# Three edits to the attention half of a fused GateLoop and SwiGLU kernel: another queue for the first rotated q rows, later gate loads, and a scan per chunk and tile

## The chip, the cores and the metric

The kernel runs on one core of one Trainium2 chip. That core has TensorE (matrix products into PSUM), VectorE, ScalarE (activation functions, with tables that must be loaded), GpSimd, SyncE (which here only issues DMAs) and 16 DMA engines. The engines run at once, each through its own list of instructions in order, and wait for one another by semaphores. The metric is the device time of one execution in microseconds (us); lower is better.

## The reference, cut to what matters

A gated linear recurrence with complex gates, for 4 sequences of 768 steps with 8 heads of 48 features, and then a feed-forward network on its 3072 rows of 384. All inputs are float32 or, for the weights, wider numbers that the kernel narrows itself.

```python
mag = np.sqrt(a_re * a_re + a_im * a_im)
scale = np.minimum(mag, 0.999) / (mag + 1e-06)
a_re_n, a_im_n = (a_re * scale, a_im * scale)
for t in range(S):                                   # S = 768
    ar, ai = (a_re_n[:, :, t, :, None], a_im_n[:, :, t, :, None])
    new_re = ar * S_re - ai * S_im
    new_im = ar * S_im + ai * S_re
    kv = np.einsum('bhd,bhe->bhde', k[:, :, t], v[:, :, t])
    S_re, S_im = (new_re + kv, new_im)
    y[:, :, t] = np.einsum('bhd,bhde->bhe', q[:, :, t], S_re)
# ... y becomes x, 3072 x 384
xn = x / np.sqrt(np.mean(x * x, axis=-1, keepdims=True) + 1e-06) * rms_g
g = xn @ w_gate                                      # 384 x 1536
(g * (1 / (1 + np.exp(-g))) * (xn @ w_val)) @ w_out  # 1536 x 384
```

## The kernel before

The time axis is cut into 24 chunks of 128 steps. In a chunk, the running product of the gates is a magnitude and a phase: q is multiplied by the magnitude and turned by the phase, k is divided and turned, and then the chunk is ordinary attention, scores of 96 x 128 blocks masked with a triangle, plus a state that carries from chunk to chunk. Gates are prepared in *units*: units 0 and 1 have one chunk each, the other eleven have two. Rotated rows of q and k come out of VectorE with features of all heads mixed over 128 partitions, and are moved by DMAs (tile `ks`, `qs`, `k`, `q` to `kr`, `qr`) to a layout with one head's features on 96 partitions.

The program is emitted by a small list scheduler: each *lane* is a generator of steps with an engine, an estimated duration and the things it needs; at every turn the step that could begin first is emitted, with the lane's `late` added as a handicap and a table switch on ScalarE counted as extra. So a constant can reorder all engines. What is emitted is a fixed order for each engine.

```python
def begin(self, step, late):
    ...
    at = max(ready + self.HOP, self.clock.get(engine, 0.0))
    return at + (more["late"]() if "late" in more else late), at
# ... in run():
    switch = self.TABLE if table and self.table not in table else 0.0
    if best is None or found[0] + switch < best[0]:
        best = found[0] + switch, found[1], switch, lane
```

The loads of a unit's gates and rows, all on SyncE's queue but for the first two `im`:

```python
def load_gates():
    for u, (first_, m) in enumerate(units):
        for name, ap in (("re", a_re), ("im", a_im)):
            aside = u < 2 and name == "im"
            ...
            yield step("ACT" if aside else "SP", 0.0 if aside else 3 * order.ISSUE,
                       earlier(u, "moved3", 2) + ([("q", 1)] if u == 2 else []),
                       ..., mb=0.2 * m, ends=[(name, u)])
```

The gates of a unit: ScalarE and VectorE in turn; `w` holds the squared magnitudes, `p` their running products in each chunk:

```python
def products():
    wc = w.rearrange("p j (c t) -> p (j c) t", t=C)
    some = starts[:, 0:ND * m]                       # zeros, but for the first of each chunk
    nc.vector.tensor_copy(out=some[:, :, 0:1], in_=wc[:, :, 0:1])
    nc.vector.memset(wc[:, :, 0:1], 0.0)
    nc.vector.tensor_tensor_scan(out=flat(p), data0=flat(w), data1=flat(some),
                                 initial=0.0, op0=ALU.mult, op1=ALU.add)
# ... then roots, q * p, k * r, phase sums by scans, sine and cosine, and the rotation:
for i, (o, x, f) in enumerate((("ks", "k", s), ("qs", "q", s), ("k", "k", y), ("q", "q", y))):
    ... tt(t[o], t[x], f)                            # ends ("rot%d" % i, u)
```

The moves; ScalarE issues those of q for units 0 and 1:

```python
def move(i, ...):
    name, rows = ("kr", "qr")[i % 2], (1 - i // 2) * D
    queue = nc.scalar if u < ASIDE and i % 2 else nc.sync
    for j in range(ND):                              # ND = 3
        queue.dma_start(out=two[name][rows + j * L:rows + (j + 1) * L],
                        in_=t[("ks", "qs", "k", "q")[i]][:, j])
```

Weights come in 18 pieces of 768 KB on GpSimd's queue (`fetch`). A buffer is free again when VectorE has converted the piece before; GpSimd also waits for the piece two before to land (a copy into `behind`), and for the moved rows of units 0 and 1 ahead of pieces 3 and 4. Three operations of VectorE and one of ScalarE convert a piece (`narrow`). GpSimd also computes the power -0.5 of the row means (`rs`). TensorE fills gaps that the scheduler expects early on with matmuls on constants (`busy`), which keep its clock up and count for nothing.

The last part is `feed_forward`: for each of 12 groups of two chunks 12 tile pairs (`gv_ps`, 3 + 3 products) and then the output products (`out_ps`).

Of the kernel before, what the change touches and what calls it, by code (L numbers as in the profile page):

```python
# [24 lines left out]
ALU = mybir.AluOpType  # L25
# [3 lines left out]
P = 128  # L29
C = 128  # L30
# [15 lines left out]
class Order:  # L46
# [40 lines left out]
    def run(self):  # L87
        while self.lanes:
            best = None
            for lane in list(self.lanes):  # L90
                if lane[2] is None:
                    lane[2] = next(lane[0], None)
                    if lane[2] is None:
                        self.lanes.remove(lane)
                        continue
                found = self.begin(lane[2], lane[1])
                if found is None:
                    continue
                table = lane[2][4].get("table")
                switch = self.TABLE if table and self.table not in table else 0.0  # L100
                if best is None or found[0] + switch < best[0]:
                    best = found[0] + switch, found[1], switch, lane
            if best is None:
                assert not self.lanes, [x[2][:3] for x in self.lanes]
                return
            _, at, switch, lane = best
            engine, us, _, emit, more = lane[2]
            lane[2] = None
            self.gap = 0.0
            if engine == "PE" and (self.fill is None or self.fill not in self.ends):  # L110
                self.gap = min(at - self.clock.get("PE", 0.0), self.MOST)
                if more.get("fills") and self.gap > 1.5:
                    self.dense = self.WARM
            emit()
            pool, n = more.get("takes", (None, 0))
            if n:
                self.free[pool] = sorted(self.free[pool])[n:]
            if switch:
                self.table = more["table"][-1 if self.table == "silu" and "sigmoid" in more["table"] else 0]
            if engine == "PE":  # L120
                if at - self.clock.get("PE", 0.0) > self.GAP and not (more.get("fills") and self.gap):
                    self.dense = 0.0
                slow = self.dense < self.WARM
                self.dense += us if more.get("dense") else 0.0
                us = us * (1.9 if slow else 1.0)
            self.clock[engine] = end = at + us + switch
            if "mb" in more:
                queue = "POOL" if engine == "POOL" else "SP"
                self.moved[queue] = max(self.moved.get(queue, 0.0), at + 0.4) + more["mb"] / self.RATES[queue]
                end = self.moved[queue] + self.LAND  # L130
            end += more.get("then", 0.0)
            for k in more.get("ends", ()):
                self.ends[k] = end
            if "gives" in more:
                self.free[more["gives"]].append(end)


def step(engine, us, needs, emit, **more):
    return engine, us, needs, emit, more
# [429 lines left out]
def fast(tc, ctx, qT, kT, v, a_re, a_im, w_gate, w_val, w_out, rms_g, out, H, bad):  # L569

    nc = tc.nc
# [6 lines left out]
    ND = DM // P  # L578
    NF = DF // P
    UC = 2  # L580
    T = UC * C

    units = [(0, 1), (1, 1)] + [(n, UC) for n in range(2, N, UC)]
    NU = len(units)
    slots = [(0, 1)] + [(u,) for u in range(2, NU)]
# [17 lines left out]
    order = Order()  # L603
# [11 lines left out]
    def flat(x):  # L615
        return x.rearrange("p j t -> p (j t)")
# [15 lines left out]
    def earlier(u, what, by=1):  # L632

        k = max(u - 1, 0) - by
        return [(what, w) for w in slots[k]] if k >= 0 else []
# [23 lines left out]
    def filled(name, shape, value):  # L659
        t = consts.tile(shape, FP32, name=name)  # L660
        nc.gpsimd.memset(t, value)
        return t
# [21 lines left out]
    zero = filled("zero", [P, 1], 0.0)  # L684
    halfpi = filled("halfpi", [P, 1], PI / 2)
    round_ = filled("round_", [P, 1], ROUND)
    starts = filled("starts", [P, ND * UC, C], 0.0)
    causal = filled("causal", [C, C], 1.0)
    nc.gpsimd.affine_select(out=causal, in_=causal, pattern=[[1, C]], compare_op=ALU.is_ge,
                            fill=0.0, base=0, channel_multiplier=-1)  # L690
# [27 lines left out]
# [4 lines that stand above are left out]
                if (u, name) == (0, "im"):  # L722
                    order.ends[name, u] = 8.0
                    continue
                yield step("ACT" if aside else "SP", 0.0 if aside else 3 * order.ISSUE,
                           earlier(u, "moved3", 2) + ([("q", 1)] if u == 2 else []),
                           lambda name=name, ap=ap, u=u, q=nc.scalar if aside else nc.sync: gate(name, ap, q, u),
                           mb=0.2 * m, ends=[(name, u)])

# [23 lines left out]

    BEHIND = {3: ("piece", 7)}
    CHECK = 6
    LATE = 0.9
    WO = 1

    def gates(some):
        def E(engine, us, needs, emit, *names, **more):
            if u > 1:
                more["late"] = lambda: 0.1 if ("piece", 11) in order.ends else 0.2
            return step(engine, us, needs, emit, ends=names, **more)

        act_ = nc.scalar.activation
        for u in some:
            first_, m = units[u]
            t = UN[u]  # L770
            n1 = ND * m * C
            K = lambda x, u=u: (x, u)
# [5 lines left out]

            yield E("ACT", ac_us(n1), [K("re"), BEHIND.get(u)] + earlier(u, "rot"), begin, K("s0"))
            re, im, s, w, y, r, p, ks, qs = (t[x] for x in ("re", "im", "s", "w", "y", "r", "p", "ks", "qs"))  # L780
# [18 lines left out]

            def products():  # L800
                wc = w.rearrange("p j (c t) -> p (j c) t", t=C)
                some = starts[:, 0:ND * m]
                nc.vector.tensor_copy(out=some[:, :, 0:1], in_=wc[:, :, 0:1])
                nc.vector.memset(wc[:, :, 0:1], 0.0)
                nc.vector.tensor_tensor_scan(out=flat(p), data0=flat(w), data1=flat(some),
                                             initial=0.0, op0=ALU.mult, op1=ALU.add)

            yield E("DVE", 0.25 + n1 / 480, [], products, K("p2"))

            yield E("DVE", tt_us(n1), [K("abs")], lambda: tt(re, re, y))  # L810
            yield E("DVE", tt_us(n1), [], lambda: stt(im, re, 2.0, im, ALU.subtract, reverse0=True), K("tan"))
# [45 lines left out]
            for i, (o, x, f) in enumerate((("ks", "k", s), ("qs", "q", s), ("k", "k", y), ("q", "q", y))):  # L857
                more = [K("sin"), K("cos"), K("checked")]
# [3 lines left out]
    ASIDE = 2  # L862

    def move_rows():
        for u, (first_, m) in enumerate(units):
            t, two = UN[u], {}

            def move(i, t=t, u=u, two=two, first_=first_, m=m):
                name, rows = ("kr", "qr")[i % 2], (1 - i // 2) * D
                queue = nc.scalar if u < ASIDE and i % 2 else nc.sync  # L870
                if i < 2:
                    two[name] = sized(unit, name, H, m, p=D2)
                for j in range(ND):
                    queue.dma_start(out=two[name][rows + j * L:rows + (j + 1) * L],
                                      in_=t[("ks", "qs", "k", "q")[i]][:, j])
                for n in range(m) if i == 3 else ():
                    w = slice(n * C, (n + 1) * C)
                    U[first_ + n].update(k=two["kr"][:, :, w], q=two["qr"][:, :, w])

            for i in range(4):  # L880
                aside = u < ASIDE and i % 2
                yield step("ACT" if aside else "SP", 0.3 if aside else 3 * order.ISSUE,
                           [("rot%d" % i, u), ("y", units[u - 1][0] - 1) if u > 1 else None],
                           lambda i=i, move=move: move(i), mb=0.2 * m, then=order.MOVE,
                           ends=[("moved%d" % i, u)] + [("moved", u)] * (i == 3))
# [23 lines left out]
    parts = []  # L909
# [64 lines left out]
    def narrow(some):  # L974
# [3 lines left out]
        for i in some:  # L978
# [21 lines left out]
            def total(to=to.bitcast(I32), part=part):  # L1000
                tt(to, part["t"], to, ALU.add)

            more = dict(late=lambda i=i: (0.2 if i < 2 * NW else 0.3 if ("xT", 3) in order.ends else WO)
                        if ("rot", 1) in order.ends else LATE)
            yield step("ACT", 0.05 + ac_us(n), [("raw", i)], share, ends=[("share", i)], **more)
# [239 lines left out]
    order.lane(finish())  # L1245
    order.lane(scores(), 0.01)
    order.lane(load_gates(), 0.02)
    order.lane(load_rows(), 0.03)
    order.lane(move_rows(), 0.02)
# [1 line left out]
    order.lane(feed_forward(range(0, NG, 2)), 0.02)  # L1251
    order.lane(feed_forward(range(1, NG, 2)), 0.03)
    order.lane(gates([0]), 0.05)
    order.lane(gates(range(1, NU)), 0.2)
    order.lane(gains(), 0.1)
    order.lane(fetch(), 0.2)
    order.lane(narrow(range(0, len(parts), 2)), 0.3)
    order.lane(narrow(range(1, len(parts), 2)), 0.3)
    order.lane(small(), 0.5)
    order.fill = ("up", 1)  # L1260
# [7 lines left out]
    for to, in_, limit, op in ((ok[:, 0:ne], ends.rearrange("p u j c -> p (u j c)"), P_MIN, ALU.is_ge),  # L1268
# [9 lines left out]
                            op0=ALU.mult, op1=ALU.add)  # L1278
# [49 lines left out]
```

## Time and profile before

| | |
|---|---|
| time, median of 3 (lowest to highest) | 802.27 us (801.06 to 804.44) |
| span of the profiled execution | 798.4 us |
| busy: TensorE / VectorE / ScalarE / GpSimd | 735.0 / 424.3 / 341.7 / 43.5 us |
| first matmul | 26.84 us |
| first feed-forward tile; third | 71.35; 85.88 us |
| scores of chunk 2; of chunk 4 | 102.66; 171.43 us |
| last output product ends | 791.5 us |
| granted TensorE clock, mean | 0.977 |

The page sums busy time by engine and by slices of the span; the trace answers questions by time, and gives for each instruction how long its engine was idle before it and what ended that. TensorE does most of the work, so what is to be read is where it is not working on something useful, and what released it there. In names such as `s_ps<-qr,kr` the output stands left and the inputs right; s_ps are scores, kt_ps the transposed keys, state_ps the carried state, y_ps the attention's output.

### The profile page before, as it was taken

How to read it: one execution, taken by the hardware profiler on the slowest of the kernel's cores; microseconds unless marked ns; L12 is line 12 of the kernel's file. 1: busy time of each engine (PE TensorE's matmuls, PEld its weight loads, DVE VectorE, ACT ScalarE, POOL GpSimd, SP SyncE). 2: the span in 40 equal slices, each digit the busy share in tenths (PEclk: the TensorE clock that was granted, in tenths of full speed). 3: DMA queues.
4: the chain of work that ended last, by engine and by line, in shares of the span. 5: the costliest groups of instructions: out<-in, count | busy, mean ns of one | idle time of the engine just before them, and what ended most of it. 6: DMA issues, size and time to landing. Idle time of an engine off the chain costs nothing.

```text
span 798.4 us, 11801 instructions
## 1 busy us (share of the span) xinstructions
PE 735.0 (92%) x4728; PEld 589.0 (74%) x4728; DVE 424.3 (53%) x762; ACT 341.7 (43%) x548; POOL 43.5 (5%) x83
## 2 busy tenths in 40 slices
PE   0558989969999999999999999999999999999996
PEld 0345776857688977878878987779887778876783
DVE  4759678848395776657484756758212303320130
ACT  6455276645566647365537557454111101110110
POOL 3010122101000000000000000000000000000000
PEclk9968999989999999999999999999999999999999
DMA  8692992690847438290927556094700114301510
GB/s 225 85 220 65 156 260 80 104 193 12 117 93 84 95 44 156 38 141 12 163 37 94 96 66 112 27 175 119 99 1 1 60 50 128 119 10 51 177 40 24
DMA packets 99775, 76.46 MB, mean 96 GB/s; under 512 B 39041, under 2 KB 90497, under 8 KB 99713
## 3 DMA queue, kind: packets, MB, share of 16 engines
q1 hardware_dynamic: 93760, 60.30, 41.4%
q0 software_dynamic: 3360, 14.16, 6.3%
q10 hardware_dynamic: 2592, 1.18, 1.0%
q8 instruction: 39, 0.64, 0.4%
q14 instruction: 24, 0.19, 0.1%
HBM read 51.98 MB, written 4.76 MB: 71 GB/s over the span
## 4 chain that ended last, share of the span: by engine, by line
PE 82%; DMA 6%; DVE 4%; issue 3%; POOL 1%; ACT 0%; SPq 0%; ACTq 0%; POOLq 0%; DVEq 0%
PE gv_ps L1201 43%; PE out_ps L1225 23%; PE s_ps L1053 5%; PE y_ps L1125 5%; PE state_ps L1096 3%; DMA qr<-q 2%; PE kt_ps L1074 2%; DMA qr<-qs 1%; DMA im<-in_a_im_dram 1%; DMA kr<-k 1%; PE gv_ps L642 1%; PE ss_ps L1163 1%; POOL rs L1160 0%; DVE k L610 0%; PE ss_ps L1151 0%
## 5 line engine op out<-in xcount | busy, mean ns | idle before, releaser
L1201 PE MATMUL gv_ps<-xT,wg 128*128 128x256 f32 x864 | 213.4, 383 | 0.0
L1201 PE MATMUL gv_ps<-xT,wv 128*128 128x256 f32 x864 | 210.0, 379 | 0.0
L1225 PE MATMUL out_ps<-wo,hT 128*128 128x384 f32 x576 | 192.9, 488 | 0.0
L1201 PEld LDWEIGHTS gv_ps<-xT,wg 128*128 128x128 f32 x864 | 163.2, 192 | 27.6 <-issue 4.0
L610 DVE TENSOR_TENSOR hT<-gv_ps,hT 128x256 f32<-128x256 f32 x144 | 60.3, 422 | 226.5 <-ACT hT L1205 226.0
L1201 PEld LDWEIGHTS gv_ps<-xT,wv 128*128 128x128 f32 x864 | 164.1, 190 | 22.4
L1225 PEld LDWEIGHTS out_ps<-wo,hT 128*128 128x128 f32 x576 | 107.3, 190 | 67.6 <-issue 0.6
L1205 ACT ACTIVATE hT<-gv_ps 128x256 f32<-128x256 f32 x144 | 54.7, 383 | 234.8 <-PE gv_ps L1201 234.6
L1053 PE MATMUL s_ps<-qr,kr 96*128 96x128 f32 x384 | 51.6, 291 | 13.2 <-DMA im<-in_a_im_dram 7.9
L1053 PEld LDWEIGHTS s_ps<-qr,kr 96*128 96x128 f32 x384 | 48.7, 204 | 15.9 <-DMA im<-in_a_im_dram 8.2
L1160 POOL TENSOR_TENSOR rs<-ssq,mhalf 128x1 f32<-128x1 f32 x24 | 18.3, 764 | 558.6 <-DVE ssq L1155 558.6
L1234 ACT COPY ot<-out_ps 128x384 f32<-128x384 f32 x24 | 11.5, 479 | 74.0 <-PE out_ps L1225 74.0
L1096 PE MATMUL state_ps<-vz,kt 128*96 128x48 f32 x320 | 31.1, 252 | 9.1 <-ACT kt L1078 9.1
L1096 PEld LDWEIGHTS state_ps<-vz,kt 128*96 128x96 f32 x320 | 30.7, 170 | 11.1 <-POOL behind L966 9.7
L1058 DVE TENSOR_TENSOR am<-s_ps,causal 128x512 f32<-128x512 f32 x48 | 31.6, 683 | 12.8 <-PE s_ps L1053 12.5
L613 DVE SCALAR_TENSOR_TENSOR xT<-y_ps,gcol,rb 128x128 f32<-128x128 f32 x72 | 20.7, 343 | 26.4 <-ACT rb L1168 18.6
L1205 ACT ACT_TABLE_LOAD x25 | 32.1, 1283 | 0.4
L1050 PE MATMUL s_ps<-ks,ident 128*128 128x384 f32 x14 | 7.3, 692 | 26.8 <-DVE ks L610 26.8
L1078 ACT COPY kt<-kt_ps 128x384 f32<-128x384 f32 x40 | 17.2, 480 | 24.6 <-PE kt_ps L1074 24.6
L1125 PE MATMUL y_ps<-am,vz 128*32 128x128 f32 x768 | 26.7, 281 | 0.0
L1050 PEld LDWEIGHTS s_ps<-ks,ident 128*128 128x128 f32 x14 | 3.8, 279 | 29.7 <-issue 29.2
L1125 PEld LDWEIGHTS y_ps<-am,vz 128*32 128x32 f32 x768 | 20.3, 112 | 3.2 <-issue 1.5
(121 smaller groups left out, 742.4 us busy)
## 6 DMA issues: line engine op xcount, KB each, us to landing
k<-in_k_dram SPq DMA_DIRECT2D x24, 192.0 KB, 4.2
q<-in_q_dram SPq DMA_DIRECT2D x24, 192.0 KB, 4.4
vz<-in_v_dram SPq DMA_DIRECT2D x24, 192.0 KB, 5.1
raw<-in_w_out_dram POOLq DMA_DIRECT2D x6, 768.0 KB, 7.3
out_dram<-ot SPq DMA_DIRECT2D x24, 192.0 KB, 1.9
raw<-in_w_gate_dram SPq DMA_DIRECT2D x6, 768.0 KB, 5.1
raw<-in_w_val_dram SPq DMA_DIRECT2D x6, 768.0 KB, 4.6
raw<-in_w_out_dram SPq DMA_DIRECT2D x6, 768.0 KB, 4.5
```

Source lines behind the costliest of these rows:

```text
L610: nc.vector.tensor_tensor(out=o, in0=x, in1=y, op=op)
L613: nc.vector.scalar_tensor_tensor(out=o, in0=x, scalar=c, in1=y, op0=op0, op1=op1, **kw)
L1053: nc.tensor.matmul(u["s_ps"][a][:, h], lhsT=u["k"][:, a * HH + h], rhs=u["q"][:, a * HH + h], start=True, stop=True)
L1058: nc.vector.tensor_tensor(out=u["am"][a], in0=u["s_ps"][a], op=ALU.mult, in1=causal.unsqueeze(1).to_broadcast([C, HH, C]))
L1074: nc.tensor.transpose(u["kt_ps"][a][:, h], u["k"][:, a * HH + h], ident[0:D2, 0:D2])
L1078: nc.scalar.copy(out=u["kt"][a], in_=u["kt_ps"][a])
L1096: nc.tensor.matmul(u["st_ps"][:, h], lhsT=u["kt"][h // HH][:, h % HH], rhs=u["v"][:, h, 0:D], start=True, stop=True)
L1125: nc.tensor.matmul(u["y_ps"][32 * p:32 * (p + 1), i // 4], lhsT=columns(left, i, odd), rhs=right(2 * (i // 3) + odd), start=side == 0 and ...
L1160: nc.gpsimd.tensor_tensor(out=u["rs"], in0=u["ssq"], in1=mhalf, op=ALU.pow)
L1201: nc.tensor.matmul(ps[:, i], lhsT=w_[:, f * P // FW, d, cols], rhs=t["xT"][:, d], start=d == 0, stop=d == ND - 1)
L1205: nc.scalar.activation(out=t["hT"][:, f], in_=t["gv", f][:, 0], func=AF.Silu)
L1225: nc.tensor.matmul(t["o_ps", i], lhsT=t["hT"][:, f, i * C:(i + 1) * C], rhs=wo[:, f], start=f == 0, stop=f == NF - 1)
```

## The change

It has three parts and some constants. The moves of q of units 0 and 1 are issued by GpSimd instead of ScalarE, so that ScalarE has no DMAs among its activations. The gates of unit u are loaded once the scores of the first chunk of unit u - 2 are done, and no longer once that unit's rows are expected to be moved, so that they do not travel with rows that are waited for. The running products are one scan for each chunk and tile that starts from 1, without the copy, the memset and the tile `starts`. The constants change the handicaps of some lanes, count 0.7 of a table switch, and let unit 3's gates begin behind weight piece 11 instead of 7.

```diff
-                if best is None or found[0] + switch < best[0]:
-                    best = found[0] + switch, found[1], switch, lane
+                if best is None or found[0] + 0.7 * switch < best[0]:
+                    best = found[0] + 0.7 * switch, found[1], switch, lane
 ...
-    starts = filled("starts", [P, ND * UC, C], 0.0)
 ...
                 yield step("ACT" if aside else "SP", 0.0 if aside else 3 * order.ISSUE,
-                           earlier(u, "moved3", 2) + ([("q", 1)] if u == 2 else []),
+                           [("s", units[slots[u - 3][-1]][0])] if u > 2 else [("q", 1)] if u == 2 else [],
 ...
-    BEHIND = {3: ("piece", 7)}
+    BEHIND = {3: ("piece", 11)}
-    LATE = 0.9
+    LATE = 0.6
 ...
             if u > 1:
-                more["late"] = lambda: 0.1 if ("piece", 11) in order.ends else 0.2
+                more["late"] = lambda: 0.1 if ("piece", 11) in order.ends else 0.1
 ...
-                some = starts[:, 0:ND * m]
-                nc.vector.tensor_copy(out=some[:, :, 0:1], in_=wc[:, :, 0:1])
-                nc.vector.memset(wc[:, :, 0:1], 0.0)
-                nc.vector.tensor_tensor_scan(out=flat(p), data0=flat(w), data1=flat(some),
-                                             initial=0.0, op0=ALU.mult, op1=ALU.add)
-            yield E("DVE", 0.25 + n1 / 480, [], products, K("p2"))
+                pc = p.rearrange("p j (c t) -> p (j c) t", t=C)
+                for i in range(ND * m):
+                    nc.vector.tensor_tensor_scan(out=pc[:, i], data0=wc[:, i], data1=zero.to_broadcast([P, C]),
+                                                 initial=1.0, op0=ALU.mult, op1=ALU.add)
+            yield E("DVE", ND * m * (0.07 + C / 480), [], products, K("p2"))
 ...
-                queue = nc.scalar if u < ASIDE and i % 2 else nc.sync
+                queue = nc.gpsimd if u < ASIDE and i % 2 else nc.sync
 ...
-                yield step("ACT" if aside else "SP", 0.3 if aside else 3 * order.ISSUE,
+                yield step("POOL" if aside else "SP", 3 * order.ISSUE,
 ...
-    order.lane(gates(range(1, NU)), 0.2)
+    order.lane(gates(range(1, NU)), 0.1)
-    order.lane(narrow(range(0, len(parts), 2)), 0.3)
+    order.lane(narrow(range(0, len(parts), 2)), 0.1)
```

## The prediction

> **What bounds the kernel now.** I read the page's 40 slices first. TensorE (row PE) is busy nine tenths or more in nearly every slice from the ninth on; only the first eight (20 us each) have holes, and only there does the granted clock drop.
>
> ```profile
> PE   0558989969999999999999999999999999999996
> ...
> PEclk9968999989999999999999999999999999999999
> ```
>
> (The clock row counts tenths of full speed; the view of stages gives 0.66 for 40 to 60 us and 0.83 for 160 to 180 us.) The second view is that of busy time by stage, cut at the places where TensorE starts something new (columns: stretch, length, busy time of PE, its weight loads, VectorE, ScalarE, GpSimd, granted clock, DMA share, GB/s):
>
> ```profile
> 0.00:26.84 26.84, 0.00 (x1) 0.03 (x1) 15.68 (x36) 17.05 (x33) 7.54 (x29) 1.00 0.70 191
> 26.84:67.34 40.50, 25.10 (x204) 18.97 (x204) 27.69 (x50) 20.14 (x30) 5.79 (x11) 0.82 0.82 166
> 67.34:85.88 18.54, 18.54 (x51) 10.88 (x52) 17.62 (x27) 7.16 (x10) 0.75 (x2) 0.85 0.18 27
> 102.66:171.43 68.77, 59.07 (x402) 49.36 (x403) 51.73 (x86) 42.79 (x62) 10.83 (x16) 0.93 0.69 158
> 171.43:791.60 620.17, 618.29 (x4010) 498.21 (x4010) 303.20 (x553) 248.25 (x403) 14.59 (x20) 1.00 0.44 80
> ```
>
> From 171.43 us TensorE lacks work for only 620.17 - 618.29 = 1.9 us. So the time is "when does TensorE become saturated, and how much useful work has it done by then". VectorE and ScalarE count only in the first 171 us. The view of TensorE's own waits names every hole there:
>
> ```profile
> PE s_ps L1050 <- DVE ks L610: 26.8, 1, 26.8
> PE state_ps L1096 <- ACT kt L1078: 9.1, 1, 9.1
> PE s_ps L1053 <- DMA im<-in_a_im_dram: 7.9, 1, 7.9
> ```
>
> The 26.8 us are the first unit's gates, up to the first rotation. The 9.1 us end with ScalarE's copy of the transposed keys. Why ScalarE was late is in its timeline (ACTq is the same engine issuing a DMA; in brackets the idle time before, and who ended it):
>
> ```profile
> 29.51 3.02 ACTq L874 DMA_DIRECT2D qr<-q  x3
> 32.58 0.61 ACT L843 ACTIVATE w<-re,round__99 128x384 f32<-128x384 f32 x1 [2.25 <-DMA qr<-qs]
> 38.63 6.16 ACTq L874 DMA_DIRECT2D qr<-q  x3
> 44.84 0.84 ACT L777 ACTIVATE s<-re 128x768 f32<-128x768 f32 x1 [5.67 <-DMA qr<-qs]
> 48.47 0.84 ACT L1078 COPY kt<-kt_ps 128x384 f32<-128x384 f32 x2
> ```
>
> ScalarE issues unit 0's and 1's q moves itself, and while the third `qr<-q` issue waits for an earlier move to land, the activations behind it wait too: 2.25 and 5.67 us. The last is the SyncE timeline around the third hole (160 to 171 us):
>
> ```profile
> 155.46 2.33 SPq L874 DMA_DIRECT2D qr<-q  x3
> 158.40 2.39 SPq L674 DMA_DIRECT2D re<-in_a_re_dram  x3
> 161.19 7.74 SPq L674 DMA_DIRECT2D im<-in_a_im_dram  x3
> ```
>
> Unit 3's rotated rows leave until 157.8 us and land with unit 5's gates, 0.79 MB that nobody needs yet, at 171.4 us.
>
> **What the Trainium skill says.** "DMA: Bandwidth & Descriptors", section "Issuing engines are not separate DMA queues": transfers started from different engines run on the same 16 DMA engines, and issuing from several saves only the sequencer's issue time. So GpSimd's queue will not make the moves land faster; what it gives is ScalarE's time, and the trace agrees that this is the large item (6.16 us for three issues that took 1.9 us without a wait). "SBUF — State Buffer", section "SBUF: two separate sides": GpSimd writes the descriptors of its own DMAs, and is locked out while VectorE runs an operation in a mode with two ports. In this trace GpSimd's 18 weight issues lie between 0.72 and 0.92 us, many beside a busy VectorE, so I take 0.77 us and no stall. "TensorE: Matmul & The Clock Gate", section "What's actually happening": after an idle window of some 3.4 us the array runs at half clock. The trace agrees: the 16 score matmuls after the 7.9 us hole took 3.74 us, and 1.85 us elsewhere. No page gives the cost of a scan.
>
> **The change part by part.**
>
> *Scan.* Now a two-chunk unit costs copy 0.39, memset 0.06 and scan 1.76, from 58.14 to 60.46 us: 2.3 us. The new form is six scans of 128; a scan of that size (the phase sums, 128x128) takes 0.40 us and three in a row 1.05 us, so 2.1 us. VectorE wins 0.2 us a unit, and 0.2 to 0.3 us in each of the first two, where it is on the path once or twice: 0.5 us, which VectorE spends again on `q<-q,p` of unit 1, now ahead of unit 0's rotation (0.47 us). Unit 0's rows are thus rotated at 28.0 us as before, and the first scores start at 36 us, as before: **0 us**.
>
> *q moves on GpSimd.* I walked the queues of the new program with the durations above. The sums of unit 1 end at 29.2 us, ScalarE rounds at once, and unit 1's rotation ends at 34.3 instead of 37.2 us. ScalarE then squares unit 2's gates, loads a table and reaches the copy of the keys at 39 instead of 48.5 us; the first state starts at 40.5 instead of 49.1 us (two fillers stand ahead of it). GpSimd issues unit 1's q from 33.3 to 38.3 us, and with the 4.4 to 4.8 us that such moves took to land, unit 1's scores start at 43 us. y 0, state 1 and y 1 follow to 52.3 us. Squares, sum, GpSimd's root (1.26) and the spread then took 4.1 us, and end at 57 us. Fillers, 3.6 us, hide VectorE's xT (done at 58.7), so the first feed-forward tile starts at 60.6 instead of 71.35 us. But the next thing is weight piece 3, which VectorE converts only after unit 2's rotation. Before, that took from xT (69.5) to 86.0, 16.5 us; the new order puts two operations of 0.95 us more after xT: 58.7 + 16.5 + 1.8 = 77 us. TensorE resumes real tiles (third and on) at 77 instead of 85.9 us: **9 us**.
>
> *Gates behind scores.* On SyncE the order becomes moves of a unit, then k, q, v of the next, then the gates of the one after. For unit 2 the moves are beside two weight transfers (768 KB each) as before, so scores of chunk 2 start some 91 to 93 instead of 102.66 us; the 2.8 us hole and the cold start there (2.90 against 1.85 us) may go: **1 to 2 us** more. Between chunks 2 and 4 the new order of TensorE has 24 - 7 = 17 tile pairs instead of 21 - 7 = 14 ahead of chunk 4's scores: 3 x 2.59 = 7.8 us of real work before it needs unit 3's rows. From 91 us, the old stretch without its hole (68.8 - 7.9 = 60.9) plus 7.8 brings TensorE there at 160 us, or up to 4 us sooner. Unit 3's gates now start behind piece 11; VectorE's list from there to the rotation adds up to 33 us, from about 107 to 141 us, and the moves land at 152 to 158 us without the gates behind them. So the hole of **7.9 us** is closed, and the cold scores after it give **1.9 us**.
>
> *Scheduler constants* (lane delays, 0.7 of a table switch) only reorder; the tile counts agree again from chunk 6 on (26 pairs), fillers are 20 matmuls in both, table loads 74 against 75. I give them 0.
>
> Sum: 9 + 1.5 + 7.9 + 1.9 = 20 us, 802.3 - 20 = **782 us**.
>
> **The rivals.** (1) GpSimd becomes the wait: its queue is in order, and the root of chunk 0 now stands behind a copy that waits for weight 3 to land. If it comes 5 us late, the first state's gain is half lost, and the time is 787. For it: weights take 8.3 us to land (median of the first 180 us), and VectorE's list stands in order behind that root. Against: weight 3 is issued at about 38.4 us and so lands at 46.7, and the root's input is only ready at 48.7 us, a slack of 2 us. (2) Chunk 4's hole stays: unit 3 starts later behind piece 11, and three wo pieces (12 and 13 ahead of it) sit in VectorE's list. If rows come at 165 us, some 5 to 7 of the 9.8 us are lost: 789. For it: slack of only about 2 to 8 us by my sums; against: the gates no longer share the landing. (3) The head is hidden anyway: weight conversion, which paces pieces 6 to 11, gives back what units 0 to 2 win: 792 to 798. Against: each weight's fetch waits for a conversion that itself comes 9 us sooner. (4) Later units, with gates loaded later, open new holes after 171 us; before, they had 1.9 us in all, and attention is over at 635 us, so slack is there: at most a few us.
>
> **Range and chances.** Losses of rivals 1 and 2 together give 795; everything as well as my walk of the queues allows (24 us) gives 778, and some 10 us beyond is not excluded, as fillers and the first wait are static. I take 769 to 797. The 2% mark lies at 786: 4 us from the centre, so faster 0.62, within 2% 0.33, slower 0.05.
>
> **What would show it.** Right: no `qr` issue on ScalarE and its copies of `kt` at 39 to 41 us; the wait `state_ps <- ACT kt` under 2 us; third tile at 75 to 79 us; no wait of `s_ps` on a gate load near 160 us; a clock of 1.0 from 160 us on. Wrong: a wait for GpSimd's root over 3 us, a `qr` landing over 8 us on GpSimd's queue in the first 45 us, or a `s_ps` wait over 4 us at chunk 4.

## The result and the profile after

The changed kernel takes **788.9 us** (median of four runs, 787.86 to 789.91) against 801.66 us for the kernel before (four runs): ratio **0.984 [0.980, 0.987]**. The prediction was 782 us with a range of 769 to 797; the gain is 12.8 us where 20 were predicted. Lines of the program after stand two below those of the kernel before (scores are L1051, not L1053).

The page's row of TensorE and its clock in 40 slices, kernel after:

```profile
PE   0479898999999999999999999999999999999996
...
PEclk9988999999999999999999999999999999999999
```

The clock is pulled down less in the ninth slice, where TensorE had its third hole (0.91 of full speed for 160 to 180 us, 0.83 before), and from the eighth slice on TensorE is busy nine tenths or more. The view of busy time by stage (columns as before: stretch, length, busy PE, weight loads, VectorE, ScalarE, GpSimd, clock, DMA share, GB/s):

```profile
28.39:58.54 30.15, 22.65 (x201) 16.84 (x201) 25.43 (x50) 18.76 (x28) 12.06 (x23) 0.93 1.05 186
...
94.95:169.56 74.61, 69.31 (x443) 56.93 (x444) 53.96 (x91) 43.25 (x65) 8.78 (x16) 0.95 0.66 155
169.56:781.00 611.44, 609.13 (x3975) 489.58 (x3973) 301.57 (x578) 247.36 (x403) 16.66 (x20) 1.00 0.42 80
```

The first row is the stretch that took 40.50 us before, from the first product to the last spread ahead of the feed-forward; it now takes 30.15. The second is that between chunk 2's and chunk 4's scores: it was 68.77 us and is *longer* now, 74.61, although it has no hole at its end. The view of TensorE's waits says which holes went and which came:

```profile
PE s_ps L1051 <- DMA qr<-q: 6.2, 2, 3.1
PE ss_ps L1161 <- POOL rs L1158: 4.0, 3, 1.6
PE gv_ps L642 <- DVE hT L610: 3.0, 1, 3.0
```

The 9.1 us for `kt` and the 7.9 us put down to a load of gates are gone. The 6.2 us for `qr<-q` are those of the first scores (3.06; before, 2.5 us there ended with the move `dec<-ends`) and the one at chunk 2 (3.11; 2.8 before); what is new is the wait of 3.0 us that ends with VectorE's `hT`.

**The head.** ScalarE's timeline around the first transposed keys, kernel after:

```profile
41.78 0.48 ACT L1076 COPY kt<-kt_ps 128x384 f32<-128x384 f32 x1 [1.33 <-PE kt_ps L1072]
```

ScalarE is idle 1.33 us ahead of the copy: it now waits for TensorE, at 41.78, where it came late at 48.47. GpSimd's timeline (POOL rows at L872 are issues of moves, L958 of weights; three issues in the first row):

```profile
37.07 1.57 POOL L872 DMA_DIRECT2D qr<-q  x3
...
51.57 0.67 POOL L1158 TENSOR_TENSOR rs<-ssq,mhalf 128x1 f32<-128x1 f32 x1 [1.66 <-DVE ssq L1153]
```

An issue of a move takes 0.53 to 0.76 us, and the root starts 0.1 us after VectorE's `ssq` (51.33 + 0.15): the first rival, a queue held up by weights, did not come.

**From chunk 2 to chunk 4.** TensorE's timeline, kernel after:

```profile
94.95 3.40 PE L1051 MATMUL s_ps<-qr,kr 96*128 96x128 f32 x16 [3.11 <-DMA qr<-q]
...
159.14 5.40 PE L642 MATMUL gv_ps<-causal,ident 128*128 128x512 f32 x8 [3.01 <-DVE hT L610]
...
169.56 1.95 PE L1051 MATMUL s_ps<-qr,kr 96*128 96x128 f32 x16
```

The scores of chunk 4 (last line) wait for nothing and run warm. But the line above is a filler, a matmul whose result nobody reads, which the scheduler puts where it expects TensorE to be idle so that the clock stays up. Here it comes *after* 3.01 us of waiting and takes 5.40 us itself. Who made it wait stands in the timelines of VectorE and ScalarE:

```profile
156.80 0.96 DVE L613 SCALAR_TENSOR_TENSOR wo<-raw,wo 128x768 int32<-128x768 int32 x1 [4.08 <-ACT wo L987]
...
158.67 0.75 DVE L610 TENSOR_TENSOR hT<-gv_ps,hT 128x256 f32<-128x256 f32 x2
```

```profile
149.68 0.84 ACT L776 ACTIVATE s<-re 128x768 f32<-128x768 f32 x1 [2.14 <-DVE qs L610]
...
155.90 0.87 ACT L987 ACTIVATE wo<-raw 128x768 f32<-128x768 uint32 x1
156.78 1.28 ACT L1203 ACT_TABLE_LOAD   x1
158.08 0.66 ACT L1203 ACTIVATE hT<-gv_ps 128x256 f32<-128x256 f32 x2
```

ScalarE works through unit 4's gates from 149.68 to 155.9 us, and only then makes its share of `wo` and the silu of two finished tiles. VectorE stands 4.08 us in front of that share, its products `hT` stand behind it, and the PSUM tile that TensorE needs next is read by them: TensorE's wait ends with `hT`. Before, the stretch had fillers too, but shorter ones:

```profile
126.76 4.44 PE L642 MATMUL gv_ps<-causal,ident 128*128 128x512 f32 x6
```

They stood behind a wait of 1.83 us; in their place there are now 1.02 us of filler behind 0.97 us.

The difference of the two profiles, 798.4 - 787.9 = 10.5 us, in steps (a tile pair is 2.59 us, and three more of them now stand ahead of chunk 4):

| reached | before | after | gain so far, equal work | gain of the step |
|---|---|---|---|---|
| product of weight piece 3 | 87.17 | 79.06 | 8.11 | 8.1 |
| scores of chunk 2 | 102.66 | 94.95 | 7.71 | -0.4 |
| scores of chunk 4 | 171.43 | 169.56 | 1.87 + 7.77 = 9.64 | 1.9 |
| scores of chunk 6 | 223.76 | 212.43 | 11.33 | 1.7 |
| end of the span | 798.4 | 787.9 | 10.5 | -0.8 |

The first product started 1.55 us later in this profile than in that of before, ahead of anything that the steps speak of. The profiled run of the changed kernel is at the slow end of its runs (789.65 us), that of the kernel before at the fast end of its own (800.14 us), so the medians lie 2 us further apart than the profiles.

### The profile page after: what moved, and what is told of

Its sections match the earlier page's. It is cut to its first block, busy times and chain, and to the rows that moved or that the text cites. A ratio compares the mean times of both kernels' runs of the same rounds, so it can differ in the third digit from the quotient of the medians.

```text
span 787.9 us, 11853 instructions
## 1 busy us (share of the span) xinstructions
PE 734.1 (93%) x4728; PEld 585.9 (74%) x4728; DVE 424.8 (54%) x795; ACT 339.1 (43%) x548; POOL 49.5 (6%) x94
## 4 chain that ended last, share of the span: by engine, by line
PE 80%; DMA 5%; DVE 4%; ACT 4%; issue 1%; POOL 1%; SPq 0%; DVEq 0%; ACTq 0%; POOLq 0%
PE gv_ps L1199 40%; PE out_ps L1223 23%; PE s_ps L1051 5%; PE y_ps L1123 5%; PE state_ps L1094 3%; DMA qr<-q 2%; PE kt_ps L1072 2%; DMA hT<-in_w_val_dram 1%; PE gv_ps L642 1%; DMA raw<-in_w_val_dram 1%; PE ss_ps L1161 1%; ACT L781 1%; DMA kr<-ks 1%; DVE im L613 0%; ACT y L781 0%
## 5 line engine op out<-in xcount | busy, mean ns | idle before, releaser
L1051 PE MATMUL s_ps<-qr,kr 96*128 96x128 f32 x384 | 49.3, 283 | 6.5 <-DMA qr<-q 6.2
L1051 PEld LDWEIGHTS s_ps<-qr,kr 96*128 96x128 f32 x384 | 46.8, 196 | 8.5 <-issue 4.0
L1022 DVE TENSOR_REDUCE least__117<-raw 128x1 f32<-128x768 f32 x18 | 17.0, 944 | 16.3 <-DMA raw<-in_w_out_dram 16.3
```

The costliest lines, as they stand in the source:

```text
L1022: nc.vector.tensor_reduce(out=least_[:, i:i + 1], in_=words(raws.pop(i))[1].bitcast(FP32), axis=mybir.AxisListType.X, op=ALU.min, apply_ab ...
L1051: nc.tensor.matmul(u["s_ps"][a][:, h], lhsT=u["k"][:, a * HH + h], rhs=u["q"][:, a * HH + h], start=True, stop=True)
```

## The experiments

**Each part alone on the kernel before.** The edits are the hunks of the diff shown above: the queue and step of `move` (queue), the condition of the gates' loads (gates), the loop of scans with its estimate (scan), and the six scheduler constants (constants).

> The kernel before with one part of the change: q moves of units 0 and 1 on GpSimd's queue. Theory A (ScalarE's freedom moves the whole head forward, and the rest follows): third feed-forward tile at 77 to 79 us instead of 85.9, the hole before chunk 4's scores stays about as it was, and the time falls by 7 to 9 us, to 793 to 795. Theory B (the conversion of the weights paces the head anyway and gives it back): third tile 83 us or later, time 799 to 802.

> The kernel before with one part: gates of unit u loaded behind the scores of unit u - 2. Theory A (the gates delay the rows they travel with): unit 3's last q rows land 3 us or more sooner than 171.4 us, the hole of 7.9 us shrinks by as much, time 795 to 799. Theory B (the rows share the DMA engines with the weight pieces, and it is those that delay them): landing within 2 us of before, the hole stays at 6 us or more, time 800 to 803.

> The kernel before with one part: the running products by one scan a chunk and tile. Theory A (off the path, 0.2 to 0.3 us of VectorE a unit): time 800 to 802.5. Theory B (three instructions fewer in front of each unit's roots shorten the first chain and the one of unit 3): first scores 0.5 to 1 us sooner and time 797 to 799.5.

> The kernel before with the scheduler constants alone (handicaps, 0.7 of a table switch, unit 3 behind piece 11). It puts 24 instead of 21 tile pairs ahead of chunk 4's scores. Theory A (the constants close the hole with real work): the wait of chunk 4's scores for rows under 2 us, time 793 to 797. Theory B (they only reorder, as the prediction said): time 800 to 803, with a wait of another kind in the place of the hole.

| kernel | median us | ratio to before [95%] |
|---|---|---|
| queue alone | 798.4 | 0.997 [0.995, 0.998] |
| gates alone | 802.6 | 1.001 [0.999, 1.002] |
| scan alone, with its new estimate | 811.9 | 1.013 [1.010, 1.016] |
| constants alone | 800.5 | 0.998 [0.997, 0.999] |

The factors multiply to 1.009, and the whole change is 0.984: no part brings the gain, and together they bring more than their product. TensorE's timeline with the queue alone:

```profile
79.68 2.86 PE L1201 MATMUL gv_ps<-xT,wv 128*128 128x256 f32 x6 [1.95 <-DVE wv L610]
98.97 3.75 PE L1053 MATMUL s_ps<-qr,kr 96*128 96x128 f32 x16 [4.83 <-DMA re<-in_a_re_dram]
167.26 3.78 PE L1053 MATMUL s_ps<-qr,kr 96*128 96x128 f32 x16 [6.79 <-DMA re<-in_a_re_dram]
```

Piece 3's product comes at 79.68, 7.5 us sooner: the head is this part's doing. But half of it is lost at chunk 2, whose rows TensorE now reaches earlier than they land (98.97 is 3.7 us sooner), so the time that Theory A gave, 793 to 795, did not come. The changed kernel hardly loses there, with the same head (79.06), because unit 2's rows leave SyncE some 3 us sooner; queue alone, then the changed kernel:

```profile
83.93 2.33 SPq L874 DMA_DIRECT2D qr<-q  x3
```

```profile
80.98 2.42 SPq L872 DMA_DIRECT2D qr<-q  x3
```

The hole at chunk 4 stays with the queue alone, 6.79 us. With the gates alone it stays too (6.91 us), although no gate is loaded ahead of the wait any more. (That profile is of the fastest of its 20 runs, 6.4 us below their median, with a `kt` wait of 4.3 us instead of 9.1; its early times are not typical.) The view of DMA issues (136 to 170 us; KB each, median us from issue to landing) shows unit 3's rows landing nearly as long after their issue as before, where they took 13.7 us; first with the gates alone, then in the changed kernel:

```profile
qr<-q SPq DMA_DIRECT2D x3, 128.0 KB, 13.0
```

```profile
qr<-q SPq DMA_DIRECT2D x3, 128.0 KB, 6.2
```

What differs is the weights that GpSimd issues meanwhile, 768 KB each. With the gates alone the q rows leave SyncE from 148.5 to 150.8 us, beside two weights that land at 158.8 and 162.8 us (the second and third line; the first landed at 146.4). In the changed kernel they leave from 155.6 to 157.4 us; the weight ahead of them had landed at 151.4 us, and the next was issued behind them:

```profile
139.77 0.72 POOL L960 DMA_DIRECT2D raw<-in_w_out_dram  x1 [11.38 <-ACT s L853]
146.23 0.72 POOL L960 DMA_DIRECT2D raw<-in_w_out_dram  x1 [5.14 <-DVE hT L610]
150.61 0.72 POOL L960 DMA_DIRECT2D raw<-in_w_out_dram  x1 [3.47 <-DVE wo L613]
```

```profile
146.05 0.72 POOL L958 DMA_DIRECT2D raw<-in_w_out_dram  x1 [10.06 <-ACT w L850]
158.32 0.72 POOL L958 DMA_DIRECT2D raw<-in_w_out_dram  x1 [10.75 <-DVE wo L613]
```

TensorE's timeline with the constants alone:

```profile
106.92 2.02 PE L1053 MATMUL s_ps<-qr,kr 96*128 96x128 f32 x16 [2.87 <-DMA qr<-q]
169.57 5.40 PE L642 MATMUL gv_ps<-causal,ident 128*128 128x512 f32 x8 [3.01 <-DVE hT L610]
179.99 1.95 PE L1053 MATMUL s_ps<-qr,kr 96*128 96x128 f32 x16
```

Here chunk 4's hole is closed: three more tile pairs lie ahead of it, and unit 3's rows land after 7.2 us, still with the next gates issued right behind them. And the new wait for `hT` with its filler is already there. The price is a head that is 4 us later (chunk 2 at 106.92).

**The scan: the instruction or its estimate.** The scheduler's estimate of the running products changes with the scan. The new scans were run on the kernel before with the old estimate:

```diff
-            yield E("DVE", ND * m * (0.07 + C / 480), [], products, K("p2"))
+            yield E("DVE", 0.25 + n1 / 480, [], products, K("p2"))
```

> The kernel before with the new scans, but with the scheduler still told the old duration (0.25 + n/480), so that every instruction of TensorE stands in the same order as before. Theory A (the scan itself costs nothing; what made it 10 us slower alone was the new order that its new estimate brought): time 799 to 803. Theory B (six short scans are worse than one long): time 808 to 813, and VectorE's stretch from the scan to the roots is longer in the trace.

800.0 us, ratio 0.999 [0.998, 1.001]. TensorE's list is then the same as before, instruction for instruction, so the six scans cost nothing that can be seen, and the 10 us of the scan part are the new order alone. With that order TensorE's scores wait at chunk 6 as well as at chunk 4. (The profile puts both waits down to a load of gates; scores read only moved rows, and the last rows landed at 170.25 and 219.14 us.)

```profile
170.80 3.75 PE L1051 MATMUL s_ps<-qr,kr 96*128 96x128 f32 x16 [4.42 <-DMA re<-in_a_re_dram]
219.27 3.44 PE L1051 MATMUL s_ps<-qr,kr 96*128 96x128 f32 x16 [4.58 <-DMA re<-in_a_re_dram]
```

**The whole change without one part.** Without the new condition of the gates' loads:

```diff
-                           [("s", units[slots[u - 3][-1]][0])] if u > 2 else [("q", 1)] if u == 2 else [],
+                           earlier(u, "moved3", 2) + ([("q", 1)] if u == 2 else []),
```

> The changed kernel with the gates' old condition back; TensorE's order is the same up to chunk 6. Theory A (with a faster head the gates behind unit 2's rows begin to cost): scores of chunk 2 start 3 to 5 us later than the 95.0 us of the changed kernel, time 791 to 795. Theory B (the gates never mattered, as alone): scores of chunk 2 at 94 to 96.5 us, time 787 to 790.

789.2 us, 0.984 [0.982, 0.987], as with it: this part is worth nothing here. Without the constants (all six as before):

> The changed kernel with the scheduler constants of before (queue, gates and scans stay changed). TensorE's list has 22 tile pairs ahead of chunk 4's scores instead of 24. Theory A (the parts only work together: the head comes from the queue, the closed hole at chunk 4 from the constants' three extra pairs): the head stays (third tile's piece 3 at 79 to 80 us), the wait at chunk 4 is back with 4 to 8 us, and the time is 793 to 799 us. Theory B (the constants are worth nothing, as the prediction said; the queue and the new place of the gates' loads close the hole by themselves): wait at chunk 4 under 2 us, time 786 to 791.

807.4 us, 1.006 [1.004, 1.008]: slower than the kernel before, and outside what either theory gave. TensorE's timeline of this kernel:

```profile
80.16 1.56 PE L1199 MATMUL gv_ps<-xT,wv 128*128 128x256 f32 x6 [1.96 <-DVE wv L610]
99.50 3.75 PE L1051 MATMUL s_ps<-qr,kr 96*128 96x128 f32 x16 [6.56 <-DMA qr<-q]
167.31 2.36 PE L1051 MATMUL s_ps<-qr,kr 96*128 96x128 f32 x16 [3.80 <-DMA qr<-q]
215.26 3.75 PE L1051 MATMUL s_ps<-qr,kr 96*128 96x128 f32 x16 [4.50 <-DMA out_dram<-ot]
```

The head is there (80.16), and then chunks 2, 4 and 6 wait for their rows: 6.56, 3.80, 4.50 us. Unit 2's q rows leave SyncE from 84.86 us, 3.9 us later than in the changed kernel, so at chunk 2 the constants are worth 4.5 us (99.50 and 94.95). The hole at chunk 4 came back as Theory A had it, if smaller; the size missed in part because the hole at chunk 6, the mark of the new estimate with old constants, came with it. That left the question whether the constants only mend what the new estimate broke. With all of the change but the old estimate:

```diff
-            yield E("DVE", ND * m * (0.07 + C / 480), [], products, K("p2"))
+            yield E("DVE", 0.25 + n1 / 480, [], products, K("p2"))
```

> The changed kernel with all its instructions, but the running products keep the old estimate of their time in the scheduler (0.25 + n1/480 instead of ND*m*(0.07 + C/480)), which alone had moved the time by 10 us when the constants were those of before. Theory A (queue and constants together are the whole gain; with the new constants the list is the same up to chunk 6, 24 and 26 tile pairs ahead of chunks 4 and 6, whichever estimate is used): 786 to 791 us, third tile, chunk 2 and chunk 4 where they are in the changed kernel, to 1 us. Theory B (the constants were set for the new estimate and pay only with it): 794 to 800 us, with a wait of more than 3 us at one of chunks 4 to 8.

788.8 us, 0.984 [0.980, 0.988], the same as with the new estimate. So the estimate's 10 us arise under the old constants only. The gain needs the constants; it can do without the gates' new place and without the new estimate, each left out by itself (both at once were not run, nor the old constants with the old estimate and the other parts).

**GpSimd's queue, or only ScalarE's relief.** The first q moves put on SyncE, which issues the k moves already:

```diff
-                queue = nc.gpsimd if u < ASIDE and i % 2 else nc.sync
+                queue = nc.sync
...
-                yield step("POOL" if aside else "SP", 3 * order.ISSUE,
+                yield step("SP", 3 * order.ISSUE,
```

> The changed kernel with the first q moves on SyncE's queue instead of GpSimd's. Theory A (what counts is that ScalarE is free, whichever queue takes them): copies of the keys at 41 to 44 us, time within 3 us of 789. Theory B (SyncE's queue, with the k moves in it, is too slow to issue all twelve): first and second scores 3 us or more later than 38.9 and 46.3 us, time 793 to 797.

798.3 us, 0.996 [0.995, 0.997]. SyncE's and TensorE's timelines:

```profile
43.09 3.02 SPq L897 DMA_DIRECT2D decay<-dec  x2
```

```profile
37.87 2.50 PE L1051 MATMUL s_ps<-qr,kr 96*128 96x128 f32 x16 [3.04 <-DMA kr<-ks]
47.57 2.05 PE L1051 MATMUL s_ps<-qr,kr 96*128 96x128 f32 x16 [1.32 <-DMA decay<-dec]
...
67.59 0.56 PE L1149 MATMUL ss_ps<-ones,sq 128*128 128x1 f32 x2 [9.35 <-DVE sq L610]
```

The keys are copied at 41.0 us, as with GpSimd: ScalarE's relief alone gives that. SyncE issues 24 moves from 27.65 to 43.0 us and only then the decay's; still the first scores come 1.06 us sooner and the second only 1.27 us later than in the changed kernel. The loss comes after that, where the sum of squares waits 9.35 us, and it stands in VectorE's timeline:

```profile
66.37 0.56 DVE L610 TENSOR_TENSOR sz<-sz,decay 96x384 f32<-96x384 f32 x1 [3.08 <-DMA decay<-dec]
```

VectorE takes unit 2's gates and a weight first and then waits for the next decay, which SyncE issues from 59.15 us, behind loads. The scheduler gave every engine another order for this queue, TensorE's too from the second scores on. So neither theory holds whole: free ScalarE, and the keys are in time, but whether SyncE could have taken the moves in the changed kernel's order this run does not tell.

**The wait and the fillers at 159 us.** First the five fillers of the second feed-forward group were left out (they compute nothing):

```diff
-                    busy(flat(ps))
+                    if g != 1:
+                        busy(flat(ps))
```

> The changed kernel without the five filler matmuls on constants in group 1 (one at 120.7 us, four at 159 us); the order of everything else is the same. Theory A (the four fillers, 5.4 us, are pure loss, as unit 3's rows have landed by 163 us): scores of chunk 4 at 163 to 165.5 us instead of 169.6, time 783 to 785.5. Theory B (the fillers only fill a wait for rows): scores of chunk 4 within 2 us of 169.6, with a wait for a DMA ahead of them, time 787.5 to 790.

785.9 us, **0.982 [0.979, 0.984]**, the lowest median of all; but its runs (784.62 to 787.72) overlap those of the kernel without the gates part on the same chip (786.89 to 790.11), and its interval overlaps that of the changed kernel, so the times alone do not settle it. TensorE's timeline:

```profile
159.27 1.56 PE L1200 MATMUL gv_ps<-xT,wg 128*128 128x256 f32 x6 [2.98 <-DVE hT L610]
164.55 1.95 PE L1051 MATMUL s_ps<-qr,kr 96*128 96x128 f32 x16
```

The wait for `hT` is the same, and after it TensorE takes real tiles at once, reaches chunk 4 at 164.55 and finds its rows there. From chunk 2 to chunk 4 it took 71.05 us instead of 74.61, though this run began the stretch at a lower clock (3.75 us for chunk 2's scores); from chunk 3's scores (101.85 us here, 101.70 in the changed kernel) it took 62.70 instead of 67.86. So in these two profiles 5.2 us of the fillers were loss; the medians lie 3.0 us apart, and the fillers do not take 5.40 us in every run (the last section). Rows that landed at 163.3 us would not have let TensorE come much sooner. Then unit 4's gates were held behind piece 15, so as to take away the wait itself:

```diff
-    BEHIND = {3: ("piece", 11)}
+    BEHIND = {3: ("piece", 11), 4: ("piece", 15)}
```

> The changed kernel; unit 4's gates may start on the engines only behind piece 15 of the weights' conversion, so that they no longer stand ahead of ScalarE's share of wo and of the silu. 24 tile pairs stay ahead of chunk 4's scores, 12 output matmuls instead of 6, and 16 fillers instead of 20. Theory A (the 3.0 us wait on hT and the 5.4 us of fillers at 159 us come from unit 4's gates on ScalarE): both go, chunk 4's scores at 162 to 165 us with at most 1 us of wait, time 782 to 785. Theory B (that wait is VectorE's own backlog, or unit 4's late gates open a hole at chunk 6 instead): the sum of waits after 155 us stays above 4 us, time 787 to 793.

792.0 us, 0.988 [0.984, 0.992]. The four times fall into two pairs, 789 and 794 to 795 (mean granted clock 0.985 and 0.979), for which no run here gives a cause; the profile is of the faster pair. Its TensorE:

```profile
164.57 1.95 PE L1051 MATMUL s_ps<-qr,kr 96*128 96x128 f32 x16
...
176.33 0.49 PE L1161 MATMUL ss_ps<-ident,rs 128*128 128x128 f32 x2 [1.92 <-POOL rs L1158]
178.69 0.56 PE L1149 MATMUL ss_ps<-ones,sq 128*128 128x1 f32 x2 [1.87 <-DVE sq L610]
```

At 159 us there is no wait and no filler, and chunk 4 is reached at 164.57 without waiting, with six more output products behind it (4.03 us of work): the cause named by Theory A is right. The time is Theory B's: the gain goes into two waits that were not there before (1.92 and 1.87 us, inside the norm of chunks 4 and 5), and into a lower clock. The view of busy time by stage, chunk 4's scores to chunk 6's, this kernel and then the changed one:

```profile
164.57:212.60 48.03, 44.13 (x302) 32.06 (x301) 29.64 (x52) 24.84 (x37) 2.56 (x2) 0.93 0.58 95
```

```profile
169.56:212.43 42.87, 42.87 (x302) 30.56 (x301) 31.14 (x59) 23.45 (x34) 1.91 (x2) 1.00 0.44 70
```

TensorE is idle for 48.03 - 44.13 = 3.9 us and at clock 0.93, and reaches chunk 6 no sooner than the changed kernel, with one tile pair more done. At the end of the span 0.7 us of the profiled gain is left.

**Chunk 2's rows beside weights.** Weight 7, and with it those behind it in GpSimd's queue, was fetched only after unit 2's rows had gone:

```diff
-    BACK = {3: (0, "moved3"), 4: (1, "moved3")}
+    BACK = {3: (0, "moved3"), 4: (1, "moved3"), 7: (2, "moved3")}
```

> The changed kernel with weight 7's fetch held back until unit 2's rotated rows have been issued. Theory A (the rows of unit 2 land after 11.8 us because two weights of 768 KB are under way beside them): the q rows land within 8 us of their issue, at 89 to 91 us, and the wait at chunk 2 is under 1.5 us; what weight 7 and those behind it lose by it is to be read from the waits that follow, so the time may be anything from 784 to 795. Theory B (the landing is set by the rows' own pattern or by their queue): it stays at 10 to 12 us.

The view of DMA issues (70 to 106 us; KB each, median us from issue to landing), kernel after and then this one:

```profile
qr<-q SPq DMA_DIRECT2D x3, 128.0 KB, 11.8
```

```profile
qr<-q SPq DMA_DIRECT2D x3, 128.0 KB, 7.6
```

and TensorE's timeline of this one:

```profile
89.05 2.02 PE L1051 MATMUL s_ps<-qr,kr 96*128 96x128 f32 x16 [1.25 <-DMA k<-in_k_dram]
...
129.48 4.56 PE L642 MATMUL gv_ps<-causal,ident 128*128 128x512 f32 x10 [2.82 <-DVE hT L610]
174.87 3.15 PE L1051 MATMUL s_ps<-qr,kr 96*128 96x128 f32 x16 [4.60 <-DMA k<-in_k_dram]
```

Theory A's landing holds: 7.6 instead of 11.8 us, and chunk 2's scores are warm at 89.05, with one tile pair fewer ahead of them. It doesn't pay: 809.8 us, 1.010 [1.006, 1.013]. The weights are issued 10 us later (weight 7 at 89.74 instead of 78.92), VectorE converts them later, TensorE meets fillers and another wait for `hT`, and chunk 4's hole is back with 4.60 us. The loss is beyond the 795 that the text allowed.

## Why the prediction was right, and where it was not

The time fell into the range, 7 us above the centre; of its working, the head held, and the attribution of the rest did not. One reading was off by a slice: the third hole and its drop of the clock lie in the ninth slice of the page, not among the first eight; no sum rests on that.

*q moves on GpSimd, 9 us.* Right: 8.1, and the queue alone gives 7.5. The copies of `kt` came at 41.8 instead of 39, in part because the whole chain began 1.55 us later. Moves on GpSimd's queue landed 5.4 us (`qs`) and 7.3 us (`q`) after their issue in the head (medians), not the 4.4 to 4.8 that the walk took from ScalarE's.

*Gates behind scores, 1 to 2 us at chunk 2.* Wrong, -0.4: the wait is 3.11 us and the scores are cold (3.40 us), as before. The gates had not been what delayed those rows (13.6 us to land before, 12.9 with the gates alone); the two weights of 768 KB beside them are most of it, as holding them back showed (11.8 to 7.6 us). The Trainium skill has this in "DMA: Bandwidth & Descriptors", section "Queues, rings and completion order": each DMA engine takes turns between its queues, packet by packet, so a weight on GpSimd's queue takes its share from the rows on SyncE's as long as it is under way. The two landings agree with that; the turns themselves no run here shows.

*The hole at chunk 4, 7.9 us, and the cold scores after it, 1.9 us.* This is the step that failed, by 6 us. Its end was right: no wait at the scores, and 1.7 us for warm scores. But the working asked only when TensorE would arrive and when the rows would land. They landed at about 163 us (issued up to 157.4, 6.2 us to land), later than the 152 to 158 of the prediction, so that TensorE, had it come at 160, would have waited 3 us; and on TensorE's way there, which the prediction filled with tile pairs at 2.59 us, lay 3.01 us of wait for `hT` and 5.40 us of filler, in part in place of the 1.83 and 4.44 us of before. Of the 7.9 us, 1.9 remained. The clock of 1.0 from 160 us, one of its signs, did not come either: 0.67 from 159.14 to 164.38. The rival that named this hole gave 789, which is what came, though by another way: the rows' lateness was to cost it, and it was ScalarE's order and fillers planned from an estimate.

Its cause was wrong as well, and that the hole closed all the same was luck. The prediction gave the closing of the hole to the gates' loads, because they stood behind the rows in SyncE's list, and never looked at GpSimd's list beside it. The rows land after 13.7 us with the gates behind them and 13.0 without, where two weights are under way beside them; after 6.2 us without gates and 7.8 with them (in the change without its gates part), where only one is, issued behind them. That the weights are the cause is shown by an experiment at chunk 2; at chunk 4 it is read from these four landings. It is the constants, which were given 0, that put the weights and the three more tile pairs there. Without the gates part the time is the same, without the constants it is 18.5 us longer.

*Scan, 0.* Right for the instruction (ratio 0.999). The estimate beside it is another part, which the prediction did not price: 10 us under the old constants, nothing under the new.

*Later units.* As said, at most a few us: a wait of 1.6 us at 233 us is new, one of 1.6 us at 346 us is gone; 0.8 us are lost in all.

*What stays open.* What each of the six constants is worth by itself, what queue and constants alone give together, and what the change would be with the q moves left on ScalarE, were not run. Nor is it settled why the kernel with unit 4's gates held back has two times.

## What to carry to other kernels

Where a scheduler decides the order, a changed constant or estimate of time is a change of the program (the same edit cost 10 us under one set of constants and nothing under another), so leave parts out of the whole one at a time instead of only trying each alone. When a transfer lands late, look at what all queues have under way, not only at what stands behind it in its own. When more work is to close a hole, walk the engines that feed that work too, and look up in the trace where fillers planned from estimates really fall: behind a wait and ahead of real work they are plain loss (5.2 us between two profiles here).

## What was not expected of the hardware

The clock after a short wait is not settled by its length. After a wait of 3.0 us for `hT` the same four fillers (eight records in the trace) took 5.40 us in the changed kernel and with the constants alone (3.01 us of wait each), and 3.70 us without the gates part or with the old estimate (3.00 us each); the granted clock was 0.67 in the changed kernel and 1.00 without the gates part. Score matmuls after 2.87 us of wait took 2.02 us with the constants alone, and 2.90 after 2.81 us in the kernel before. The Trainium skill, "TensorE: Matmul & The Clock Gate", section "What's actually happening", has windows of some 3.4 us for this, which run freely, so that where a wait falls in them can differ from run to run; the scatter fits that. But it has the half clock after an idle window, and here waits of 2.4 to 3.0 us, shorter than one, were enough to lose clock at times (2.99 us for the scores after 2.41 us with the gates alone, at a clock of 0.64), and at times not.

A q move issued by GpSimd took 0.53 to 0.76 us of its queue (median 0.53), no more than on ScalarE without a wait (0.55 to 0.85), beside a VectorE that was busy (25.43 of 30.15 us).
